# An attention and feed-forward kernel: 64 bytes added behind the buffer of the attention's results

## The chip, the cores and the metric

The kernel runs on one core of one Trainium2 chip. A core has TensorE (PE, matrix products, with its weight loads shown apart as PEld), VectorE (DVE), ScalarE (ACT), GpSimd (POOL) and SyncE (SP, which issues transfers). They share a buffer memory of 128 partitions. An address in this document is a byte offset within a partition, the same in all 128. Products are written to eight banks of an accumulator memory. The metric is device time in microseconds (us), as the median of several runs.

## What is computed

Two parts follow each other. The first is attention with decay, in blocks of 64 positions, for 4 batches, 8 heads, 768 positions and 64 values a head:

```
for each block of 64 positions:
    intra = ((q_b @ k_b.T) * Dmask) @ v_b           # Dmask[i, j] = lam ** (i - j) for j <= i, else 0
    inter = (q_b * lam ** (pos + 1)) @ kv_state
    out_b = intra + inter
    kv_state = lam ** 64 * kv_state + (k_b * lam ** (63 - pos)).T @ v_b
```

The second takes the result as x, 3,072 tokens of 512 values, with float32 weights of 512 x 2048 and 2048 x 512:

```
h = maximum(x @ w_in, 0)
out = (h * h) @ w_out
```

## The kernel before

**Tiling.** Attention goes by 24 chunks of 128 positions (two blocks). The feed-forward part goes by 8 tiles of 3 chunks, 384 tokens, and inside a tile by 16 steps f = 0 to 15, each for 128 of the 2,048 inner values. A step has two groups of matmuls:

- The first group (line 465) makes h for 384 tokens. It has 12 matmuls of 128x128 weights against 128x384 values: wih by the high part of x, wih by its low part, wil by the high part, four each.
- The second group (lines 471, 472, 474) adds to three banks, one for each chunk of the tile. It has 9 matmuls with 512 columns. Here the roles are turned: slices of gh or gl (the high and low part of h squared) are the operand that is loaded first, and woh or wol stream against them.

Between the groups ScalarE and VectorE square h and split it into gh and gl (lines 479 to 486). High and low parts are there because the matmuls take a shortened float32; three products of parts stand for one full product.

**Weights.** They are loaded once, 32 loads of 512 KB, and split into wih, wil, woh, wol by ScalarE and VectorE (lines 311 to 322) during the first 126 us; afterwards all 16 x 4 parts stay in the buffer memory, 2,048 bytes each.

**Order.** A planner in the file simulates the engines with given durations, and writes each engine's instructions in the order that it found. It does not know addresses. In the first 140 us the steps of tiles 0 and 1 interleave as weights arrive. After that the tiles go one by one, and steps run in pairs: first group of f, first group of f + 1, second group of f, second group of f + 1. Attention chunks for the next tile are put between such groups (about 2 us of small matmuls, line 334), three a tile; the last tile has none beside it.

**Where things lie.** Tiles are laid out one behind the other in the order in which they are made. As the built program places them:

| what | begins at byte | within 512 |
|---|---|---|
| wih, wil, woh, wol of f = 0 to 8 (made first) | 1,152, then every 2,048 | 128 |
| gh, gl, three of each, 1,536 bytes; a slice every 512 | 74,880 to 84,096 | 128 |
| ka, qv, st and the rest | 91,264 to 146,816 | 128 for nearly all |
| xs, one tile for the results of attention | 146,816 | 384 |
| the four parts of x in it (two slots, high and low) | 146,880 to 171,456 | 448 |
| dot, wdec, lc (small tables) | 171,456 | 448, 480, 32 |
| space of the first six chunks' ka, qv, xr; later wih, wil, woh, wol of f = 9 to 15 | 171,584, then every 2,048 or 4,096 | 64 |

The first 16 floats (XOFF) of xs are not used. The last row is one stretch with two uses: six chunks of attention have loading buffers of their own there, and when these are done the weights of the seven late steps take their place (`late`, line 235).

Of the kernel before, what the change touches and what calls it, by code (L numbers as in the profile page):

```python
# [12 lines left out]
F32R = mybir.dt.float32r  # L13
# [6 lines left out]
P = 128  # L20
# [3 lines left out]
NCC = DM // P  # L24
# [10 lines left out]
N = NT * C  # L35
# [20 lines left out]
class Plan:  # L56
# [109 lines left out]
SLOTS = {  # L166
    "bank": 8, "run": 2, "x": 2, "gh": 3, "gl": 3, "g": 2, "ob": 2,
    "ka": 2, "qv": 3, "s1": 4, "xr": 1, "hold": 8, "st": 3, "m": 3, "ka0": 6, "qv0": 6, "xr0": 4}
# [6 lines left out]
XOFF = 16  # L175
# [20 lines left out]
def kernel(ctx: ExitStack, tc: tile.TileContext, ka, qv, lamx, w, out):  # L196
    nc = tc.nc
    const = ctx.enter_context(tc.tile_pool(name="const", bufs=1))
# [25 lines left out]
    make(const, [k for k in SLOTS if k not in ("bank", "x", "run") + EARLY])  # L224
    rdec = const.tile([P, NCC, C], F32, name="rdec")
    mask = const.tile([P, HC], F32, name="mask")
    xs = const.tile([P, XOFF + 2 * SLOTS["x"] * NCC * N], F32R, name="xs")
    tiles["x"] = [[xs[:, XOFF + (2 * i + t) * NCC * N:XOFF + (2 * i + t + 1) * NCC * N].rearrange("p (c i) -> p c i", c=NCC) for t in range(2)] for i in range(SLOTS["x"])]
    dot = const.tile([P, 1], F32, name="dot")
    wdec = const.tile([P, 2 * H], F32, name="wdec")  # L230
# [364 lines left out]
```

## Time and profile before

| | us |
|---|---|
| median of 3 runs | 615.11 |
| lowest, highest | 613.01, 616.09 |
| profiled execution, its own time | 614.58 |
| span of its records | 612.8 |
| TensorE busy in the span | 605.6 |
| VectorE busy | 299.1 |
| ScalarE busy | 215.0 |

The granted TensorE clock is 0.997 of full speed over the span. A line of the profile names the source line, the engine, the operation, and the tiles that it writes and reads, without their numbers: `bank<-xs,wih` is a matmul of a wih tile against x. The profile models where a matmul ends, so two matmuls seem to overlap; the distance from one start to the next tells how fast they go. A timeline merges neighbours of one kind (x8 is eight of them) and gives the start of the first.

### The profile page before, as it was taken

The numbers are of one execution on the slowest core, as the hardware profiler recorded it, in microseconds if no ns is written. First come the engines' busy times: TensorE is split into PE (matmuls) and PEld (weight loads), VectorE is DVE, ScalarE is ACT, GpSimd is POOL, SyncE is SP. The second block draws the span as 40 slices with busy tenths as digits, with TensorE's granted clock in tenths as the row PEclk, the third lists the DMA queues.
The fourth block names the chain that finished last, engine by engine and source line by source line (L and its number), as shares of the span: only waits on it lengthen the run. The fifth ranks groups of instructions, "written<-read, shape, count | busy, mean of one in ns | idle before, by whom it ended". The sixth has DMA issues, their size and how long they took to land.

```text
span 612.8 us, 12922 instructions
## 1 busy us (share of the span) xinstructions
PE 605.6 (99%) x5700; PEld 537.5 (88%) x5700; DVE 299.1 (49%) x612; ACT 215.0 (35%) x450; POOL 5.3 (1%) x10
## 2 busy tenths in 40 slices
PE   8999999999999999999999999999999999999997
PEld 4779998989989888989898988999888989889996
DVE  5899999945334344344243453334443423232223
ACT  4667777743332132322222222323122223122221
POOL 3000000000000000000000000000000000000000
PEclk9899999999999999999999999999999999999999
DMA  7747555324211011121021120112110000010001
GB/s 280 245 153 302 189 175 172 138 89 172 70 52 70 7 65 70 52 70 72 0 71 51 71 70 18 52 56 66 71 71 35 19 0 2 1 51 1 0 2 51
DMA packets 15175, 49.06 MB, mean 80 GB/s; under 512 B 1808, under 2 KB 1808, under 8 KB 15120
## 3 DMA queue, kind: packets, MB, share of 16 engines
q1 hardware_dynamic: 14976, 48.24, 22.2%
q8 instruction: 44, 0.72, 0.5%
q14 instruction: 11, 0.09, 0.0%
q10 hardware_dynamic: 144, 0.01, 0.0%
HBM read 41.96 MB, written 6.29 MB: 79 GB/s over the span
## 4 chain that ended last, share of the span: by engine, by line
PE 93%; DMA 5%; DVE 1%; ACT 0%; issue 0%; SPq 0%
PE bank L465 43%; PE bank L471 15%; PE bank L472 14%; PE bank L474 14%; PE bank L334 6%; DMA qv<-qv 2%; DMA ka<-ka 2%; DMA st<-w 1%; ACT m L311 0%; DVE m L316 0%; DVE xr L504 0%; DVE s L395 0%; DVE xr L441 0%; DVE hold L387 0%; ACT woh L320 0%; DVE m L318 0%
## 5 line engine op out<-in xcount | busy, mean ns | idle before, releaser
L465 PE MATMUL bank<-xs,wih 128*128 128x384 f32 x1024 | 200.7, 338 | 0.0
L465 PEld LDWEIGHTS bank<-xs,wih 128*128 128x128 f32 x1024 | 180.6, 188 | 6.4
L479 ACT ACTIVATE g<-bank 128x384 f32<-128x384 f32 x128 | 62.8, 491 | 275.2 <-PE bank L465 275.1
L485 DVE TENSOR_TENSOR g<-g 128x384 f32<-128x384 f32 x96 | 53.5, 558 | 212.9 <-ACT gh L484 167.4
L471 PE MATMUL bank<-woh,gh 128*128 128x512 f32 x384 | 152.3, 397 | 0.0
L472 PE MATMUL bank<-wol,gh 128*128 128x512 f32 x384 | 150.9, 393 | 0.0
L465 PE MATMUL bank<-xs,wil 128*128 128x384 f32 x512 | 110.1, 337 | 0.0
L474 PE MATMUL bank<-woh,gl 128*128 128x512 f32 x384 | 108.9, 392 | 0.0
L465 PEld LDWEIGHTS bank<-xs,wil 128*128 128x128 f32 x512 | 91.1, 188 | 0.0
L474 PEld LDWEIGHTS bank<-woh,gl 128*128 128x128 f32 x384 | 72.0, 188 | 16.5 <-DVE gl L486 0.5
L471 PEld LDWEIGHTS bank<-woh,gh 128*128 128x128 f32 x384 | 72.0, 188 | 14.6 <-ACT gh L482 0.3
L472 PEld LDWEIGHTS bank<-wol,gh 128*128 128x128 f32 x384 | 72.1, 188 | 13.4
L486 DVE TENSOR_TENSOR gl<-g,gh 128x384 fp32r<-128x384 f32 x128 | 71.1, 556 | 19.9 <-ACT gh L482 12.7
L484 ACT ACTIVATE gh<-g 128x384 fp32r<-128x384 f32 x96 | 50.4, 525 | 3.0
L387 DVE TENSOR_TENSOR hold<-bank,hold 128x256 f32<-128x256 f32 x40 | 16.8, 419 | 28.1 <-PE bank L334 24.9
L447 ACT CAST xs<-xr 128x512 fp32r<-128x512 f32 x24 | 14.9, 621 | 43.3 <-DVE xr L441 43.3
L334 PE MATMUL bank<-qv,ka 64*64 64x64 f32 x1472 | 28.2, 223 | 0.0
L334 PEld LDWEIGHTS bank<-qv,ka 64*64 64x64 f32 x1472 | 25.9, 138 | 0.9 <-issue 0.9
L363 DVE TENSOR_TENSOR qv<-qv,wdec 128x512 f32<-128x512 f32 (+1 forms) x24 | 14.2, 590 | 23.3 <-DMA qv<-qv 23.2
L334 PEld LDWEIGHTS bank<-s,qv 64*64 64x64 f32 x768 | 16.1, 135 | 10.5 <-issue 6.1
L311 ACT ACTIVATE m<-st 128x512 f32<-128x512 f32 x32 | 21.5, 673 | 7.8 <-DMA st<-w 7.7
L334 PE MATMUL bank<-s,qv 64*64 64x64 f32 x768 | 21.9, 228 | 1.2 <-DVE s L395 0.7
(46 smaller groups left out, 302.5 us busy)
## 6 DMA issues: line engine op xcount, KB each, us to landing
st<-w SPq DMA_DIRECT2D x32, 512.0 KB, 3.6
ka<-ka SPq DMA_DIRECT2D x24, 512.0 KB, 3.9
qv<-qv SPq DMA_DIRECT2D x24, 512.0 KB, 4.8
out<-ob SPq DMA_DIRECT2D x23, 256.0 KB, 2.1
out<-xr SPq DMA_DIRECT2D x1, 256.0 KB, 2.0
g<-lamx ACTq DMA_DIRECT2D x1, 12.0 KB, 4.1
```

The lines of the kernel that those rows point to most:

```text
L311: o = add("ACT", 0.56, lambda: nc.scalar.activation(at(m), words(1).bitcast(F32), AF.Abs), [o], [st, m])
L334: nc.tensor.matmul(*args, **kw, skip_group_check=True)
L387: return plan.op("DVE", tt(256), key, lambda: nc.vector.tensor_tensor(out=at(new), in0=u(t), in1=at(old), op=ALU.add), [o] + deps, [self.s ...
L447: oh = plan.op("ACT", act(512), key2, lambda: nc.scalar.copy(at(x)[0][:, :, cs], at(xr)), os_, [xr, x])
L465: nc.tensor.matmul(at(h)[:, 0:N], wt[:, cc, :], xt[:, cc, :], start=k == 0, stop=k == 3 * NCC - 1)
L471: nc.tensor.matmul(at(os_[j]), at(gh)[:, sl], woh[f], start=f == 0, stop=False)
L472: nc.tensor.matmul(at(os_[j]), at(gh)[:, sl], wol[f], start=False, stop=False)
L474: nc.tensor.matmul(at(os_[j]), at(gl)[:, sl], woh[f], start=False, stop=f == NF - 1)
L479: orr = plan.op("ACT", 0.49, key, lambda: nc.scalar.activation(at(g), at(h)[:, 0:N], AF.Relu), [o1], [h, g, run])
L484: ogh = plan.op("ACT", 0.525, key, lambda: nc.scalar.activation(at(gh), at(g), AF.Square), [orr], [g, gh])
L485: og = plan.op("DVE", 0.555, key, lambda: nc.vector.tensor_tensor(out=at(g), in0=at(g), in1=at(g), op=ALU.mult), [orr, ogh], [g])
L486: ogl = plan.op("DVE", 0.555, key, lambda: nc.vector.tensor_tensor(out=at(gl), in0=at(g), in1=at(gh), op=ALU.subtract), [og, ogh], [g, gh, ...
```

## The change

```
-    xs = const.tile([P, XOFF + 2 * SLOTS["x"] * NCC * N], F32R, name="xs")
+    xs = const.tile([P, 2 * XOFF + 2 * SLOTS["x"] * NCC * N], F32R, name="xs")
```

The tile xs grows by 16 floats, 64 bytes in each partition, at its end. The parts of x in it stay where they are. All that lies behind it moves up by 64 bytes: dot, wdec and lc, the buffers of the first six chunks, and the weights of f = 9 to 15, which now begin at 171,648 and every 2,048 bytes from there, at 128 within 512, as those of f = 0 to 8 do. No instruction is added, removed or put elsewhere in the order of any engine.

## The prediction

> **What bounds the kernel now.** I read the page's share of busy time first, then the chain of waits, the waits of all engines, and last the timeline of TensorE, in which the change's effect has to be found.
>
> ```profile
> PE 605.6 (99%) x5700; PEld 537.5 (88%) x5700; DVE 299.1 (49%) x612; ACT 215.0 (35%) x450; POOL 5.3 (1%) x10
> PE 93%; DMA 5%; DVE 1%; ACT 0%; issue 0%; SPq 0%
> ```
>
> The first row is the busy time of each engine, the second the share of each engine in the chain that ended last. TensorE sets the time: 93% of the chain is matmul, and most of what remains is the loads of the first 30 us. The waits say the same: ScalarE and VectorE wait for the matmul groups.
>
> ```profile
> ACT g L479 <- PE bank L465: 275.1, 120, 5.3
> DVE gl L486 <- PE bank L474: 1.5, 1, 1.5
> ```
>
> (Engine and line that waited, for whom; us in total, times, longest.) So what a step of the feed-forward part takes is what its 12 + 9 matmuls take one behind the other. A busy share of 99% does not say whether these go as fast as they can. For that I looked at when they start. The last tile of tokens has no attention beside it; its sixteen steps f = 0 to 15 run in pairs: first group of f, first group of f + 1, second group of f, second group of f + 1. The pair that starts at 600.43 is f = 14 and 15, since it is the last; counted back, 592.00 is 12 and 13, 583.58 is 10 and 11, 575.20 is 8 and 9, 566.94 is 6 and 7, 558.69 is 4 and 5.
>
> ```profile
> 558.69 1.55 PE L465 MATMUL bank<-xs,wih 128*128 128x384 f32 x8
> 560.08 0.86 PE L465 MATMUL bank<-xs,wil 128*128 128x384 f32 x4
> ...
> 562.85 0.39 PE L471 MATMUL bank<-woh,gh 128*128 128x512 f32 x1
> ...
> 564.90 0.39 PE L471 MATMUL bank<-woh,gh 128*128 128x512 f32 x1
> ...
> 566.94 1.55 PE L465 MATMUL bank<-xs,wih 128*128 128x384 f32 x8
> ...
> 575.20 1.55 PE L465 MATMUL bank<-xs,wih 128*128 128x384 f32 x8
> ...
> 577.28 1.57 PE L465 MATMUL bank<-xs,wih 128*128 128x384 f32 x8
> ...
> 579.39 0.40 PE L471 MATMUL bank<-woh,gh 128*128 128x512 f32 x1
> ...
> 581.48 0.39 PE L471 MATMUL bank<-woh,gh 128*128 128x512 f32 x1
> ...
> 583.58 1.57 PE L465 MATMUL bank<-xs,wih 128*128 128x384 f32 x8
> ...
> 592.00 1.57 PE L465 MATMUL bank<-xs,wih 128*128 128x384 f32 x8
> 593.41 0.86 PE L465 MATMUL bank<-xs,wil 128*128 128x384 f32 x4
> ...
> 596.23 0.39 PE L471 MATMUL bank<-woh,gh 128*128 128x512 f32 x1
> ...
> 598.33 0.39 PE L471 MATMUL bank<-woh,gh 128*128 128x512 f32 x1
> ...
> 600.43 1.57 PE L465 MATMUL bank<-xs,wih 128*128 128x384 f32 x8
> ```
>
> Columns: start in us, busy us (modelled ends; I use starts only), engine, line, what. The pair 4/5 takes 566.94 - 558.69 = **8.25 us**. The pair 10/11 takes 592.00 - 583.58 = **8.42** and the pair 12/13 600.43 - 592.00 = **8.43**. The work is the same to the instruction, and nothing waits in any of them. In the second groups the difference is plain: nine matmuls from 564.90 to 566.94 are 2.04 us, 227 ns each; from 598.33 to 600.43 they are 2.10 us, 233 ns each. In the first groups it is smaller: 24 matmuls in 562.85 - 558.69 = 4.16 us against 596.23 - 592.00 = 4.23 us, 173 against 176 ns each. A late step so loses 0.035 us in its first group and, half of (600.43 - 596.23) - (566.94 - 562.85) = 0.11, 0.055 us in its second.
>
> The border between fast and slow is where the kernel's weights come from two places. The tiles of f = 0 to 8 lie at the front of the buffer memory, each beginning 128 bytes past a multiple of 512. Those of f = 9 to 15 lie behind xs, and begin 64 bytes past one. The results gh and gl, against which the second group runs, begin at 128; x begins at 448. So before, early weights stand in one relation to their partner and late weights in another that is 64 bytes off, and the change makes them alike.
>
> **Is it the place within 512 bytes, or how far up the memory they lie?** The other operand helps here. The four halves of xs that the tiles use in turn lie right below the late weights (146,880 to 171,456 bytes), far above the early ones. The tile before the last uses the lower two halves, the last tile the upper two. A fast pair of the tile before the last (f = 1 and 2) goes from 473.51 to 481.77:
>
> ```profile
> 473.51 1.55 PE L465 MATMUL bank<-xs,wih 128*128 128x384 f32 x8
> ...
> 481.77 0.51 PE L465 MATMUL bank<-xs,wih 128*128 128x384 f32 x2
> ```
>
> That is 8.26, the same as with the upper halves. An operand streamed from high up, at 448 within 512, costs nothing extra, and the early weights are alike from byte 1,152 up to 74,880. Only at the border f = 9, where the place within 512 changes, does the time step. This is why I hold the place for the cause, though no run so far has moved it alone.
>
> **The change part by part.** It adds no instruction, removes none, and moves none on any engine; only addresses behind xs change.
>
> (1) *Late weights, from 64 to 128.* They should run like the early ones. Each tile of tokens has the pair 8/9, which takes 583.58 - 575.20 = 8.38 us, so 0.13 over 8.25; the pair 10/11, 0.17 over; 12/13, 0.18 over; and 14/15, taken as 0.17. That is 0.65 us a tile, and there are 8 tiles: **5.2 us**. The pair 8/9 needs a word. Half of it is early: f = 8. Yet its second group takes 581.48 - 579.39 = 2.09 us, not the 2.05 of f = 4 (564.90 - 562.85), 0.04 more. I take that for a carry-over from the slow group of f = 9 that runs ahead of it, which goes when f = 9 is fast. If it is something else, 8 x 0.04 = 0.3 us stay and the gain is 4.9. In the first two tiles, whose steps interleave, I charge the same per step. The other engines keep up there: the early steps already run at 8.25 us a pair beside the same ScalarE and VectorE work, and TensorE is full from 60 to 140 us, where these steps lie:
>
> ```profile
> 60.00:140.00 80.00, 80.00 (x578) 71.92 (x577) 69.12 (x137) 53.05 (x102) 0.00 (x0) 1.00 0.44 152
> ```
>
> (A stretch in us, its length, then busy us of PE, PEld, DVE, ACT, POOL; granted clock, DMA share, GB/s.) VectorE, which splits the weights, is busy 69 of 80 us there, so it is the cover that is thinnest. If the faster steps of these two tiles ran ahead of it and waited, all of their part would be lost, 2 x 0.65 = 1.3 us, which leaves 3.9 us. The nearest case is wil of f = 11:
>
> ```profile
> 98.60 0.68 DVE L322 TENSOR_TENSOR wil<-m,wih 128x512 fp32r<-128x512 f32 x1
> ...
> 101.50 0.87 PE L465 MATMUL bank<-xs,wil 128*128 128x384 f32 x4
> ```
>
> It is done at 99.28 and used at 101.50, 2.2 us later, which is more than the 1.3 that TensorE can gain in all. I take the full value.
>
> (2) *The buffers of the first six chunks, from 64 to 128.* They share the space with the late weights. Their attention matmuls, and those of later chunks whose buffers already lie at 128, compare directly:
>
> ```profile
> 32.75 0.65 PE L334 MATMUL bank<-qv,hold 64*64 64x64 f32 x32
> 33.22 1.11 PE L334 MATMUL bank<-qv,ka 64*64 64x64 f32 x64
> ...
> 306.03 0.65 PE L334 MATMUL bank<-qv,hold 64*64 64x64 f32 x32
> 306.49 1.11 PE L334 MATMUL bank<-qv,ka 64*64 64x64 f32 x64
> ```
>
> The chunk at 33 us (buffers at 64) and the one at 306 us (at 128) are equal to 0.01 us: **0**.
>
> (3) *The loads into these buffers,* on the chain for the first 30 us. In that stretch the loads of weights land in tiles at 128, the loads of ka and qv in tiles at 64:
>
> ```profile
> st<-w SPq DMA_DIRECT2D x6, 512.0 KB, 4.7
> ka<-ka SPq DMA_DIRECT2D x6, 512.0 KB, 4.5
> qv<-qv SPq DMA_DIRECT2D x6, 512.0 KB, 4.6
> ```
>
> (Tile, count, size, median us from issue to landing, stretch 0 to 30 us.) If the 0.1 to 0.2 us between them came from the place, some 6 loads one behind the other on the chain would cost up to 1.0 us; nearer lies the reading that the loads share one set of engines, so I take **0** and keep -0.5 to +1.0 for the range.
>
> (4) *wdec, lc and dot* also move by 64 bytes. VectorE and ScalarE alone touch them, beside full matmul groups (49% and 35% busy in the first row): **0**, and without that cover still less than the loads' 1.0.
>
> Sum: 5.2 us off the profiled execution's 614.58, which is 609.4. The median of the runs, 615.11, lies 0.5 above that execution, so the forecast is **609.9 us**.
>
> **The rivals.**
>
> *The height, not the place* (no change, 615.1). The late weights could be slow because they lie beyond 171,584 bytes, whatever they begin at. For it: early and late differ in height as well as in place. Against it: xs, next to them, streams without a loss, and a border exactly between xs and the late weights would be chance. A related form is that the streams of weights and of x do not meet at all and the difference has some other source. The Trainium skill speaks for that form: "TensorE: Matmul & The Clock Gate", in its step-by-step of a matmul, says that TensorE has two independent read ports to the buffer memory, so that loading the next weights takes nothing from the running matmul; and "SBUF — State Buffer", Specifications, gives a line of 16 bytes, of which 64 and 128 are both multiples. By these two nothing would change. The trace does not agree with the first, at least not as the whole story: 233 against 227 ns for the same matmul.
>
> *Only the second groups gain* (611.7). The place that counts may be one within 1024 bytes. The early weights begin at 128 within 1024 as well, but the late ones after the change at 640 (171,648 = 167 x 1024 + 640). In the second group that cannot matter: the slices of gh lie at 128 and at 640 in turn, and all run at 227 ns. In the first group x and weights keep one distance, so no row shows the other one. If the first groups keep their loss, the gain is 7 x 8 x 0.055 + 0.3 = 3.4 us. The reverse, that only the first groups gain, is 7 x 8 x 0.035 = 2.0 us, 613.1; nothing speaks for it.
>
> *The first groups collide worse* (slower, 619.0). This is the same bit at 512, with a price. There are 7 x 8 x 12 = 672 first-group matmuls with late weights. They now lose 3 ns each. If the new distance cost 14 ns, twice the 233 - 227 = 6 to 7 ns that the second groups lose today, they would lose 11 ns more, 7.3 us, against 3.4 us gained: 3.9 us slower. It decides from a loss of 3 + 3.4 / 672 = 8 ns a matmul on. Against it: both of the distances that the trace shows cost 3 ns or less in the first group, and no collision in it costs as much as 8.
>
> **How the numbers follow.** About 0.5%, 3.1 us, is what a measurement can tell here from no change. I give the forecast 0.82, no change 0.09 (0.03 of it that the streams do not meet), the second groups alone 0.05, the first groups alone 0.01, and the slower one 0.03. The forecast's own range is 608.5 to 611.5: 0.3 for f = 8, 1.3 for the two interleaved tiles, 0.5 to 1.0 for the loads, and the runs of before, which lie 2 us below and 1 us above their median. To hold eight in ten it has to reach a little beyond, over the second-groups case: 608.0 to 613.2. Faster by over 0.5% means under 612.0: the forecast nearly whole and most of the second-groups case, 0.82. Within 0.5%: 0.15. Slower: 0.03.
>
> **What would show it.** In the timeline of the last tile every pair should take 8.25 to 8.27 us, also the last three, and the nine matmuls of a late second group 2.04 to 2.06 us. The first 60 us should not move. If late second groups stay at 2.10, the height or something else was the cause. If they fall to 2.04 but 24 late first-group matmuls stay at 4.23 or grow, the 1024 case holds. If TensorE shows new idle time before late steps between 85 and 135 us, VectorE took part of the gain back.

## The result and the profile after

The changed kernel takes **610.78 us** (median of 6 runs, 610.45 to 611.28) beside 615.39 for the kernel before (6 runs). The ratio of the means is 0.9926, with a 95% interval of 0.9902 to 0.995: faster by 3 to 6 us. The forecast was 609.9 us. The profiled execution took 610.94, its span 609.2.

In the timeline of TensorE after the change, the last tile (columns as before: start us, busy us, engine, line, what):

```profile
563.88 1.55 PE L465 MATMUL bank<-xs,wih 128*128 128x384 f32 x8
...
572.13 1.55 PE L465 MATMUL bank<-xs,wih 128*128 128x384 f32 x8
...
574.21 1.55 PE L465 MATMUL bank<-xs,wih 128*128 128x384 f32 x8
...
576.29 0.39 PE L471 MATMUL bank<-woh,gh 128*128 128x512 f32 x1
...
578.34 0.39 PE L471 MATMUL bank<-woh,gh 128*128 128x512 f32 x1
...
580.38 1.55 PE L465 MATMUL bank<-xs,wih 128*128 128x384 f32 x8
...
588.63 1.55 PE L465 MATMUL bank<-xs,wih 128*128 128x384 f32 x8
...
592.80 0.39 PE L471 MATMUL bank<-woh,gh 128*128 128x512 f32 x1
594.85 0.39 PE L471 MATMUL bank<-woh,gh 128*128 128x512 f32 x1
596.89 1.55 PE L465 MATMUL bank<-xs,wih 128*128 128x384 f32 x8
```

The pair 6/7, which is early, takes 572.13 - 563.88 = 8.25 us. The pair 12/13, which is late, takes 596.89 - 588.63 = 8.26, where it took 8.43 before. Its nine matmuls from 594.85 to 596.89 are 2.04 us, 227 ns each (233 before), and its first groups 592.80 - 588.63 = 4.17 (4.23). The pair 8/9, half early and half late, takes 580.38 - 572.13 = 8.25 (8.38), and the second group of f = 8 in it 578.34 - 576.29 = 2.05 (2.09), although nothing of f = 8 has moved. No late step can be told from an early one any more.

The page's other rows stay. The busy share hardly shows the change, since a matmul that streams slowly counts as busy too:

```profile
PE 599.9 (98%) x5700; PEld 534.9 (88%) x5700; DVE 298.8 (49%) x612; ACT 215.2 (35%) x450; POOL 5.4 (1%) x10
PE 93%; DMA 5%; DVE 1%; ACT 0%; issue 0%; SPq 0%
```

### The profile page after: what moved, and what is told of

Read it like the earlier page. It is cut to its first block, busy times and chain, and to the rows that moved or that the text cites. A ratio compares the mean times of both kernels' runs of the same rounds, so it can differ in the third digit from the quotient of the medians.

```text
span 609.2 us, 12922 instructions
## 1 busy us (share of the span) xinstructions
PE 599.9 (98%) x5700; PEld 534.9 (88%) x5700; DVE 298.8 (49%) x612; ACT 215.2 (35%) x450; POOL 5.4 (1%) x10
## 4 chain that ended last, share of the span: by engine, by line
PE 93%; DMA 5%; DVE 1%; ACT 0%; issue 0%; SPq 0%
PE bank L465 43%; PE bank L471 15%; PE bank L472 14%; PE bank L474 14%; PE bank L334 6%; DMA ka<-ka 3%; DMA qv<-qv 2%; DMA st<-w 1%; DVE m L316 0%; DVE xr L504 0%; ACT m L311 0%; DVE s L395 0%; DVE xr L441 0%; DVE hold L387 0%; ACT woh L320 0%; DVE m L318 0%
```

## Where the 4.6 us came from, and what took a part back

For a number without the start of the program I take the time from the first matmul of f = 9 in tile 0 to the first of f = 14 in the last tile. Before, these start at 88.24 and 600.43 (the second row stands above in the prediction); after, at 89.14 and 596.89:

```profile
88.24 1.56 PE L465 MATMUL bank<-xs,wih 128*128 128x384 f32 x8
```

```profile
89.14 1.55 PE L465 MATMUL bank<-xs,wih 128*128 128x384 f32 x8
```

That is 512.19 against 507.75 us, 4.44 less, and the last pair adds 0.1 to 0.2. But the late steps begin 0.90 us later than before, and by that the profiled execution as a whole gains only 614.58 - 610.94 = 3.6. Some of the first loads were issued later in this execution: the one of st that was issued at 28.73 us before, at 30.89 after. Whether the change does that, the first experiments ask.

The second small loss lies near 439 us. VectorE works there on a chunk's values (line 363), whose load came late, and gl of the step is ready after TensorE wants it:

```profile
437.30 0.69 DVE L363 TENSOR_TENSOR qv<-qv,wdec 128x512 f32<-128x512 f32 x1 [1.35 <-DMA qv<-qv]
437.90 0.55 DVE L485 TENSOR_TENSOR g<-g 128x384 f32<-128x384 f32 x1
438.49 0.56 DVE L486 TENSOR_TENSOR gl<-g,gh 128x384 fp32r<-128x384 f32 x1
...
439.10 0.53 PEld L474 LDWEIGHTS bank<-woh,gl 128*128 128x128 f32 x3 [0.35 <-DVE gl L486]
```

This is the timeline of all engines after the change; the bracket is the idle time before an instruction and what ended it. Of the 0.35 us in which no weights were loaded, matmuls already issued cover a part; from f = 8 to its end this tile takes 464.89 - 431.32 = 33.57 us, the tile before it 391.89 - 358.55 = 33.34, so some 0.2 are lost. The same wait stands in every profile, 0.3 to 2.1 us of it in all, before the change too (0.5).

## The experiments

The theory was that the place of the late weights within 512 bytes, taken against the operand that they run with, sets the pace. Rivals were their height in the memory, and that the early buffers at 128 make the start slower. "Path" is the time from the first matmul of f = 9 to f = 14 of the last tile, as above.

**The same kernel again, the late weights alone, the early buffers alone.** The first has no edit. The second leaves xs as it was and puts 64 bytes ahead of the late weights only:

```
+        pool.tile([P, 16], F32, name="pad")       # in the pool "late", ahead of the weights
```

The third puts the same 64 bytes ahead of the six early chunks' buffers, and leaves the late weights at 64.

> The changed kernel once more, beside the kernel before on the same chip. In its first profile the late steps (f = 9 to 15) run like the early ones, 8.25 us a pair in the last tile, but the stretch before 60 us ends 1.4 us later than before. Theory (the place of the late weights does all of it, the later start is chance): 610.8 us, and the attention chunk that stood at 34.29 us before starts anywhere between 33.5 and 36.0. Rival (the early buffers at 128 make the loads slower): it starts at 35.5 or later again.

> Only the weights of f = 9 to 15 move from 64 to 128 within 512; the buffers of the first six chunks and the small tables stay where they were. Theory: late pairs 8.25 us as in the changed kernel, time 610 to 611 us, the same as the changed kernel. Rival (the early buffers at 128 cost some 1.2 us of start): the same pairs, but 609.4 us, and a start as early as before in every execution.

> Only the buffers of the first six chunks move from 64 to 128; the late weights stay at 64. Theory: late pairs 8.42 us as before, time as the kernel before, 615.4 us within 0.3%. Rival (early buffers at 128 slow the loads): 616.6 us.

| kernel | median us (runs) | ratio of means to before, 95% interval | first f = 9 at | path |
|---|---|---|---|---|
| before | 615.63 (17) | | 88.24 | 512.19 |
| after, first profile | 610.78 (6) | 0.9926, 0.9902 to 0.995 | 89.14 | 507.75 |
| after, again | 611.28 (6) | 0.9921, 0.9902 to 0.9941 | 88.50 | 507.59 |
| late weights alone | 611.35 (6) | 0.9935, 0.9912 to 0.9958 | 89.18 | 507.66 |
| early buffers alone | 616.33 (12) | 1.0007, 0.9992 to 1.0022 | 89.50 | 512.92 |

(The ratio of the first profile's row is to the six runs of before in the section on the result, the others to the 17 here.) The whole gain comes with the late weights, and the buffers of the early chunks do nothing that can be measured. The start does not follow the place of the early buffers. The changed kernel alone started f = 9 at 89.14 in one profile and at 88.50 in the other. With the early buffers at 64, f = 9 starts at 88.24, 89.18 and, in kernels further below, as late as 90.71; with them at 128 at 88.50, 89.14, 89.50 and 90.91. What sets the start is open. The profile of before, from which the prediction was made, happened to have the earliest start of all thirteen profiles. In the repeat the attention chunk that stood at 34.29 before is at 35.08, inside the range of the theory. The rival's 609.4 us for the late weights alone did not come; the pair 12/13 of that kernel's last tile takes 596.84 - 588.59 = 8.25 us.

The path of the early buffers alone is 0.7 us longer than before, though its late pairs are the old ones (602.42 - 593.99 = 8.43). It has more of the wait on gl:

```profile
PEld bank L476 <- DVE gl L488: 1.7, 5, 0.5
```

(Waits of that kernel, whose lines are two further down: us in total, times, longest; before it was 0.5 us, 2 times.)

From here on each kernel was run once. Its time also holds its start and its waits on gl, so the groups and pairs of the last tile are compared.

**Seven places at once.** Between the late steps' weights stands a pad of 64 bytes, so that f = 9 begins at 64, f = 10 at 128, and so on to f = 15 at 448.

> The late weights lie at seven places within 512 bytes: f = 9 at 64, 10 at 128, 11 at 192, 12 at 256, 13 at 320, 14 at 384, 15 at 448. Theory (what counts is the distance between the streamed and the loaded operand within 512 or a part of it): second groups take 233 ns a matmul at 64 and 227 at 128, and each place has a time of its own; the first groups differ too, since x is at 448 and gh at 128. If the period is 128, f = 9, 11, 13, 15 are slow and 10, 12, 14 fast. Rival (only the height in memory or the pool that they come from counts, not the place): all seven equal.

The time was 614.29 us, the path 510.43. In the last tile the first and second group took, in us: f = 9 (64) 2.11 and 2.10; f = 10 (128) 2.08 and 2.05; f = 11 (192) 2.10 and 2.08; f = 12 (256) 2.08 and 2.10; f = 13 (320) 2.11 and 2.09; f = 14 (384) 2.09 and 2.05; f = 15 (448) 2.10 for the first group. The last tile ends with another order in the second group of f = 15; in the tile before, it took 2.08 us, where the changed kernel has 2.04. The two clean second groups are at 128 and 384, and 64 (2.10) is about as slow as 320 (2.09). That points to a period of 256. A period of 128 would have made 256 like 128, and it is not. "All equal" fell too. Neighbours at different places may disturb each other in a pair, so the next kernels put all late weights at one place.

**Distance or place.** This kernel turns the relation round. gh and gl and all that lies between them and xs move by 64, late weights to 192, early weights stay; x keeps its place, since the pad that stood ahead of it is used up:

```
-XOFF = 16
+XOFF = 0
+    const.tile([P, 16], F32, name="pad_gh")        # ahead of gh
+        pool.tile([P, 32], F32, name="pad")        # in the pool "late", ahead of the weights
```

> gh and gl move from 128 to 192, the late weights from 64 to 192; the early weights stay at 128 and x at 448 (the tiles between them and the tables move by 64 with gh). In the second groups the late weights are now level with gh, and the early ones lie 64 below it, as the late ones did in the kernel before. Theory A (what counts is the distance between the streamed and the loaded operand): second groups of f = 9 to 15 take 227 ns a matmul (2.04 us a group of nine), those of f = 0 to 7 take 233 (2.10 us); time near 616 us. Rival B (what counts is where the streamed weights themselves begin): f = 0 to 8 keep 227, f = 9 to 15 are slow at 192.

Its time was 615.56 us (before, beside it, 614.23), the path 512.68. In the last tile (lines three further down):

```profile
559.78 1.55 PE L468 MATMUL bank<-xs,wih 128*128 128x384 f32 x8
...
563.95 0.39 PE L474 MATMUL bank<-woh,gh 128*128 128x512 f32 x1
...
566.04 0.39 PE L474 MATMUL bank<-woh,gh 128*128 128x512 f32 x1
...
568.14 1.55 PE L468 MATMUL bank<-xs,wih 128*128 128x384 f32 x8
...
597.36 0.39 PE L474 MATMUL bank<-woh,gh 128*128 128x512 f32 x1
...
599.44 0.39 PE L474 MATMUL bank<-woh,gh 128*128 128x512 f32 x1
...
601.48 1.57 PE L468 MATMUL bank<-xs,wih 128*128 128x384 f32 x8
```

The early second groups, f = 4 and 5, now take 566.04 - 563.95 = 2.09 and 568.14 - 566.04 = 2.10 us, 233 ns a matmul, though their weights lie where they always did. The late one at 192, f = 13, takes 601.48 - 599.44 = 2.04, 227 ns. The one before it, f = 12, takes 599.44 - 597.36 = 2.08, more than theory A named; that loss comes back below, where x stands 256 above all weights, as it does above the late weights here. The second groups' pace follows the distance between the streamed and the loaded operand, not where either begins. No row of the first profile could show that, since gh stood still.

**Late weights at 192 and at 256; x moved in place of the weights.** The first two take a pad of 128 and 192 bytes ahead of the late weights. In the third all weights are at 128 and x begins at 384:

```
-XOFF = 16
+XOFF = 0
-    xs = const.tile([P, XOFF + 2 * SLOTS["x"] * NCC * N], F32R, name="xs")
+    xs = const.tile([P, 32 + 2 * SLOTS["x"] * NCC * N], F32R, name="xs")
```

> Only the late weights move, from 64 to 192: 64 above gh in place of 64 below. Theory (distance, in a period of 256 as the scan suggests): second groups at 192 are slow, 231 ns a matmul or more, first groups like f = 11 of the scan, 2.10 us in place of 2.08; time 613 to 615 us. Rival (only 64, that is, only below gh is slow): 227 ns, time 611 us.

> Only the late weights move, from 64 to 256: 128 off gh, and 192 below x. By the scan (f = 12, with f = 13 at 320 beside it) the first groups at 256 are nearly as fast as at 128, 2.08 us, and the second ones slow, 2.09 to 2.10 us. Theory (distance within 256): the same here without a neighbour at another place, so late pairs of 8.33 to 8.38 us and 613 us. Rival (f = 12 was slowed by its neighbour f = 13 alone): 8.25 us and 611 us.

> All weights at 128 as in the changed kernel, but x begins at 384 in place of 448 (the unused floats lie behind it). Second groups don't read x. Theory (distance between x and the weights, within 256): x lies 256 above the weights, as it does above the late weights at 192, so the first groups of all sixteen f take what the late first groups take in the kernel with late weights at 192, about 2.10 us in place of 2.08, and the time is 128 x 0.02 = 2.6 us above the changed kernel, 613.5 us. Rival (only the weights' place counts): as the changed kernel, 611 us.

The pair 12/13 of the last tile with the late weights at 192:

```profile
589.80 1.57 PE L467 MATMUL bank<-xs,wih 128*128 128x384 f32 x8
...
593.99 0.39 PE L473 MATMUL bank<-woh,gh 128*128 128x512 f32 x1
...
598.11 1.57 PE L467 MATMUL bank<-xs,wih 128*128 128x384 f32 x8
```

The time was 612.19 us, below the 613 to 615 expected, the path 509.63, the pair 598.11 - 589.80 = 8.31 us. The two second groups took (598.11 - 593.99) / 2 = 2.06 us, 229 ns a matmul: less than the 231 expected, but not the 227 of the rival. 64 above gh costs about a third of 64 below, or less. Of the two first groups only the first was slow, 2.11 us. At 256 the time was 615.38 us, over the 613 expected, with a late start and a path of 511.07; the late pair of 601.31 - 592.95 = 8.36 is inside what was expected. Its second groups took 2.09 us as expected, its first groups 2.10 and 2.09 and not 2.08. So f = 12 of the scan was not slowed by its neighbour alone.

With x at 384 the time was 615.83 us, over the 613.5 expected, again with a late start (f = 9 at 90.91); the path is 510.86, 3.1 us over the changed kernel's, near the 2.6 expected. But where it is lost was not as expected. The pair 12/13 of the last tile:

```profile
593.46 1.57 PE L465 MATMUL bank<-xs,wih 128*128 128x384 f32 x8
...
595.57 1.55 PE L465 MATMUL bank<-xs,wih 128*128 128x384 f32 x8
...
597.65 0.39 PE L471 MATMUL bank<-woh,gh 128*128 128x512 f32 x1
...
599.73 0.39 PE L471 MATMUL bank<-woh,gh 128*128 128x512 f32 x1
...
601.77 1.57 PE L465 MATMUL bank<-xs,wih 128*128 128x384 f32 x8
```

The first of the two first groups takes 2.11 us and the second 2.08, as fast as ever; the first of the two second groups takes 2.08 and the second 2.04. So this distance costs nothing in a group that follows one of its kind. It costs some 27 ns whenever TensorE changes from one kind of group to the other: the first group is back at 173 ns a matmul after its first six, the second group stays at 231 ns for all nine, and the next group of the same kind runs at 173 or 227 from its first matmul on. Why it ends there no run shows. All sixteen f lose alike, the early ones too, so the rival (only the weights' place counts) fell.

**The period, and half steps.** Late weights at 384, at 96 and at 160, each by a pad ahead of them.

> Only the late weights move, from 64 to 384: 256 above gh, and 64 below x. Theory (distance within a period of 256): late pairs exactly as at 128, 8.25 us, groups 2.08, 2.08, 2.05, 2.04; time about 611 us. Rival (a period of 512 or more): some other time for a late pair, up to the 8.42 of the kernel before.

> Only the late weights move, from 64 to 96: half way, 32 below gh. Theory A (the loss grows with the distance, so half way costs about half): late pairs of 8.33 us, second groups 230 ns a matmul. Theory B (lines of 64 bytes or more count): either all of the loss, 8.42, or none, 8.25.

> Only the late weights move, from 64 to 160: 32 above gh. At 64 above (192) a late pair took 8.31 us. Theory A (the loss grows with the distance): between 8.25 and 8.31 us a pair. Theory B (lines of 64 bytes or more count): 8.25 or 8.31.

The first matmuls of f = 12 and f = 14 of the last tile, with the late weights at 384, 96 and 160:

```profile
588.42 1.55 PE L467 MATMUL bank<-xs,wih 128*128 128x384 f32 x8
...
596.67 1.55 PE L467 MATMUL bank<-xs,wih 128*128 128x384 f32 x8
```

```profile
594.13 1.57 PE L467 MATMUL bank<-xs,wih 128*128 128x384 f32 x8
...
602.55 1.57 PE L467 MATMUL bank<-xs,wih 128*128 128x384 f32 x8
```

```profile
594.69 1.58 PE L467 MATMUL bank<-xs,wih 128*128 128x384 f32 x8
...
603.13 1.58 PE L467 MATMUL bank<-xs,wih 128*128 128x384 f32 x8
```

At 384 a late pair takes 8.25 us, and the kernel 610.71 (path 507.49): the changed kernel once more. A shift of 256 changes nothing. Half steps do not halve the loss. At 96 a pair takes 8.42 (616.67 us, path 512.73), all of the loss. At 160 it takes 8.44 (617.24 us, path 512.42), more than at 192, which lies further off. For 96 theory B named the number; for 160 neither did. The loss is no smooth function of the distance.

All places tried, with the pair 12/13 of the last tile. When the late weights move, their distance to x changes together with that to gh, and x is the partner in the first groups; so the pair is given in its two parts too:

| late weights at | above gh | below x | pair, us | its two first groups | its two second groups |
|---|---|---|---|---|---|
| 64 (before) | -64 | 384 | 8.43 | 4.23 | 4.20 |
| 96 | -32 | 352 | 8.42 | 4.24 | 4.18 |
| 128 (the change) | 0 | 320 | 8.26 | 4.17 | 4.09 |
| 160 | 32 | 288 | 8.44 | 4.24 | 4.20 |
| 192 | 64 | 256 | 8.31 | 4.19 | 4.12 |
| 256 | 128 | 192 | 8.36 | 4.19 | 4.17 |
| 384 | 256 | 64 | 8.25 | 4.16 | 4.09 |

The two partners ask for different distances: the second groups are fastest with the weights level with gh or 256 above it, the first groups with the weights 64 or 320 below x. The changed kernel, with weights and gh at 128 and x at 448, gives both. No kernel tried is clearly faster than the changed one.

## Why the prediction was right, point by point

- **The border at f = 9 is the place of the weights.** Right, and shown: the late weights moved alone bring the whole gain. The rival of the height fell with the same run. On the two sentences of the Trainium skill that spoke for no effect ("TensorE: Matmul & The Clock Gate", step-by-step; "SBUF — State Buffer", Specifications), the runs decide against what was drawn from them here: seven places that are all multiples of 16 bytes give 8.25 to 8.44 us a pair.
- **What about the place counts.** The prediction spoke of the relation to the partner within 512 bytes. The relation to the partner was right (gh moved), the size was not needed: the period is 256 as far as the runs tell (128 and 384 are alike in all their groups, 64 and 320 of the scan nearly). The two rivals with a period of 1024 fell with the changed kernel itself, whose late first groups run at the early pace, 2.08 us.
- **Term 1, the sum over steps: mis-sized.** I put 5.2 us, eight times what the last tile shows. In the changed kernel's last tile that is right. In a tile with attention beside it, it is less: before, tile 6 takes 542.18 - 506.76 = 35.42 us from f = 8 to the end, after it takes 539.12 - 504.31 = 34.81, so 0.61 and not 0.65; no run separates why. Tiles 0 and 1 together gain 1.16 and not 1.3, from 88.24 to 175.89 before against 89.14 to 175.63 after. Tiles 2 to 6 together take 542.18 - 175.89 = 366.29 before and 539.12 - 175.63 = 363.49 after, 2.80 less where the sum had 5 x 0.65 = 3.25; about 0.2 of what is missing is the wait on gl near 439 us. That makes 1.16 + 2.80 + 0.64 = 4.60, with 5.2 in the sum. The four rows for tile 6:

```profile
506.76 0.62 PE L465 MATMUL bank<-xs,wih 128*128 128x384 f32 x2
...
542.18 1.03 PE L465 MATMUL bank<-xs,wih 128*128 128x384 f32 x5
```

```profile
504.31 0.97 PE L465 MATMUL bank<-xs,wih 128*128 128x384 f32 x4
...
539.12 1.20 PE L465 MATMUL bank<-xs,wih 128*128 128x384 f32 x6
```

- **The carry-over on f = 8.** The effect is right: its second group went from 2.09 to 2.05 us when only the late weights were moved. The reason given, a slow group of f = 9 ahead of it, is not enough. With the late weights at 96 the first group of f = 9 is just as slow, 581.55 - 579.43 = 2.12 us, and the second group of f = 8 behind it takes 583.60 - 581.55 = 2.05; at 160 it is the same. So a slow group need not slow the next one, and what is carried over stays open.

```profile
579.43 1.58 PE L467 MATMUL bank<-xs,wih 128*128 128x384 f32 x8
...
581.55 0.39 PE L473 MATMUL bank<-woh,gh 128*128 128x512 f32 x1
...
583.60 0.40 PE L473 MATMUL bank<-woh,gh 128*128 128x512 f32 x1
```

- **VectorE's cover.** It held where I looked for it, from 85 to 135 us: no wait of TensorE for VectorE stands there. What I had priced there came in small elsewhere, where a late load puts line 363 ahead of gl.
- **The early buffers and their loads at 0.** Right within 0.2% (0.9992 to 1.0022). "The first 60 us should not move" was no fair test: the start of f = 9 differs by 2.7 us between single profiles, and it does not follow the place of these buffers. The row of 4.7 against 4.5 and 4.6 us says nothing of the place: with all of these tiles at 128 the same three rows read 4.2, 4.8 and 4.9 in the first profile after the change, and 4.9, 4.4 and 4.8 in the second.
- **The small tables at 0.** No run moved them alone; they moved in the changed kernel and stayed in the one with the late weights alone, and the two agree (610.78 and 611.28 against 611.35). That VectorE and ScalarE alone touch them is not so: GpSimd writes wdec and lc at the start.
- **The slower rival** fell: the first groups gained too, from 4.23 to 4.17 us a pair.

## What to carry to other kernels

When the same matmul runs at two paces in one program, and nothing waits, look at where its operands begin before looking at the schedule. TensorE's busy share hides the difference; the distance from one matmul's start to the next shows it. Measure which distance between the streamed and the loaded operand is fast; here the good one was not the same for both kinds of group. Then give every buffer of one kind that distance, by a pad where a buffer breaks it, and after every change of a buffer's size look again at all that is laid out behind it.

## What the runs showed of the hardware that was not expected

- The pace of these 128x512 matmuls depends on the distance between the streamed and the loaded operand with a period of 256 bytes: 227 ns from start to start at 0 and at 256, 233 at -64, 229 at +64, 232 at +128. The period rests on these two places and on the scan. Why is open; no run here separates the reading of the two streams from other causes.
- 32 bytes off costs about as much as 64, or more: 8.42 us a pair at -32 beside 8.43 at -64, and 8.44 at +32 beside 8.31 at +64, against 8.25. The pair holds first groups too, whose distance to x changes along.
- A bad distance can cost only at changes: with x at 384, about 27 ns at each change between first and second groups, and nothing in the next group of the same kind.
